# A gated decode kernel: the product with w1 takes the weights as the moving operand, and gelu works on rows

## The chip, the cores and the metric

The kernel runs on one core of one Trainium2 chip. The metric is the device time of one execution, in microseconds (us). Before the change it was 1337.64 us, the median of 3 runs (1337.64 to 1337.76).

## The reference

Two branches read the same two tokens and are mixed by a gate. Branch A is attention over a cache of 16384 positions and 32 heads. Branch B is a small mixer and an MLP.

```python
B, S, D = 2, 1, 1024            # one position per sequence
x = A_x
g = sigmoid((x * gate_w).sum(-1, keepdims=True))
# A: q = x @ wq; softmax(q K^T / sqrt(128)) V; @ wo      K and V: 268 MB each
# B:
h  = gelu(layernorm(x) @ w1)                  # w1: 1024 x 1024
g0..g3 = the four column blocks of h, each shifted by 1, -1, 2, -2 positions
hs = concatenate([g0, g1, g2, g3]) @ w2       # w2: 1024 x 1024
x1 = x + hs
b  = x1 + gelu(layernorm(x1) @ w3) @ w4
out = g * a + (1 - g) * b
```

With S = 1 every shift moves the only position out of the sequence, so all four blocks are zero, hs is zero, and h does not reach the output. The kernel computes h all the same, and then uses a zeroed tile in its place.

## The kernel before

Everything is streamed through one ring of three buffers of 64 KB per partition: the K and V tiles of the 32 attention steps, and between them the weights. One queue carries all of these loads. A load is issued when a ring buffer becomes free.

```python
NBIG = 3
big = ctx.enter_context(tc.tile_pool(name="big", bufs=NBIG))
# ... (cut)
def issue_ready():
    while xfers:
        ring, freed_by, load = xfers[0]
        used = ring_used[ring]
        if len(used) >= ring_size[ring] and used[-ring_size[ring]] not in done:
            return
        load()                       # nc.sync.dma_start(...), always the same queue
        used.append(freed_by)
        xfers.pop(0)
```

The work on one K tile begins with 16 transposes on VectorE (DVE), each followed by four matmuls on TensorE (PE).

```python
def qk_stage(i):
    # ... (cut)
    for m in range(NM):                                   # NM = 16
        T = t_tile([P, 2, CJ, 32], FP32)
        nc.vector.transpose(out=..., in_=Kw[:, m * CW : (m + 1) * CW]...)   # L325
        for v in range(4):
            nc.tensor.matmul(S[:], lhsT=z[...], rhs=Tb[:, v // 2, :, v % 2], ...)   # L333
```

The stage that the change touches runs once, after the fifth of the 32 attention steps. It takes w1 and w2 out of one ring buffer. The reader of the profile meets it as L513 (both products), L532 (the copy of h), L491 to L504 (gelu) and L442 (the residual's matmuls, which end the stage).

```python
def linear(key, actT):                       # weights stationary, two columns moving
    w = wt.pop(key)
    R, C = w.shape[1], w.shape[2] // P       # 8 and 8
    ps = misc_psum([P, C, B])
    for c in range(C):
        for r in range(R):
            nc.tensor.matmul(ps[:, c, :], lhsT=w[:, r, :]...[:, :, c], rhs=actT[:, r, :],
                             start=(r == 0), stop=(r == R - 1))
    return ps

def st_mix():
    layernorm(xT[:], xn1T[:])
    h1 = const.tile([P, KC, B], FP32, name="h1")
    nc.vector.tensor_copy(out=h1[:], in_=linear("w1", xn1T)[:])
    gelu(h1[:], hT[:], KC)                   # hT has no reader
    nc.vector.memset(shT[:], 0.0)
    # ... (cut: raises an error if more than one position)
    nc.vector.tensor_tensor(out=x1[:], in0=xT[:], in1=linear("w2", shT)[:], op=ALU.add)
    layernorm(x1[:], xn2T[:])                # rstd by a pow on GpSimd (POOL)
    start_out(x1[:])
```

Of the kernel before, what the change touches and what calls it, by code (L numbers as in the profile page):

```python
# [10 lines left out]
FP32 = mybir.dt.float32  # L11
BF16 = mybir.dt.bfloat16
ACTF = mybir.ActivationFunctionType
ALU = mybir.AluOpType
# [9 lines left out]
def kernel(  # L24
# [15 lines left out]
    nc = tc.nc  # L40
    P = nc.NUM_PARTITIONS
    B, Sq, D = A_x.shape
# [9 lines left out]
    KC = D // P  # L52
    FC = F // P
# [8 lines left out]
    const = ctx.enter_context(tc.tile_pool(name="const", bufs=1))  # L62
# [8 lines left out]
    def misc_psum(shape, dtype=FP32):  # L71
        return mps.tile(shape, dtype, tag="misc", name="misc")
# [4 lines left out]
    def t_tile(shape, dtype, name="T"):  # L77
        return tpool.tile(shape, dtype, tag="T", name=name)
# [6 lines left out]
    wt = {}  # L85
# [53 lines left out]
    def load_first():  # L139
# [12 lines left out]
        out=perm[:].rearrange("k (h a) -> k h a", a=4),  # L152
        in_=ident_f[:].rearrange("k (a h) -> k h a", a=4),
# [26 lines left out]
    for g in range(1, 4):  # L180
        nc.vector.tensor_tensor(
            out=osel_f, in0=osel_f, in1=ident_f[:, 40 * g : 40 * g + 8], op=ALU.add
# [9 lines left out]
        out=pick[:], in_=ident_f[:].rearrange("p (g w) -> p g w", w=32)[:, :, 0:B]  # L192
# [28 lines left out]
    omg_bc = const.tile([P, B], FP32)  # L221
# [21 lines left out]
    def group(g):  # L243
        return slice(32 * g, 32 * g + B)

    def zero_rows(ps, g, width):
        nc.tensor.matmul(
            ps[32 * g : 32 * g + 32, :],
            lhsT=perm[:, 0:32],
            rhs=zero[:].to_broadcast([P, width]),  # L250
            start=True,
            stop=False,
            skip_group_check=True,
        )
# [180 lines left out]
    def start_out(x1):  # L435
        for g in range(NQ):
            zero_rows(out_acc, g, QW)
        res = const.tile([P, KC, B], FP32, name="cen")
        nc.vector.tensor_tensor(out=res[:], in0=x1, in1=over_r(omg_bc[:]), op=ALU.mult)
        for c in range(KC):  # L440
            for g in range(NQ):
                nc.tensor.matmul(  # L442
                    out_acc[group(g), c:QW:KC],
                    lhsT=res[:, c, :],
                    rhs=ident_f[:, 32 * g : 32 * g + 32],
                    start=False,
                    stop=False,
                    skip_group_check=True,
                )
# [16 lines left out]
    def layernorm(src, dst):  # L466
        part = stat.tile([P, B], FP32, name="part")
        nc.vector.reduce_sum(out=part[:], in_=src.rearrange("p r b -> p b r"), axis=AX.X)
        mean = stat.tile([P, B], FP32, name="mean")
        nc.vector.tensor_scalar(  # L470
            out=mean[:], in0=total(part[:])[:], scalar1=1.0 / D, scalar2=None, op0=ALU.mult
        )
        cen = const.tile([P, KC, B], FP32, name="cen")
        nc.vector.tensor_tensor(out=cen[:], in0=src, in1=over_r(mean[:]), op=ALU.subtract)
        sq = const.tile([P, KC, B], FP32, name="cen_sq")
        nc.vector.tensor_tensor(out=sq[:], in0=cen[:], in1=cen[:], op=ALU.mult)
        part2 = stat.tile([P, B], FP32, name="part")
        nc.vector.reduce_sum(out=part2[:], in_=sq[:].rearrange("p r b -> p b r"), axis=AX.X)
        ve = stat.tile([P, B], FP32, name="mean")
        nc.vector.tensor_scalar(  # L480
            out=ve[:], in0=total(part2[:])[:], scalar1=1.0 / D, scalar2=LN_EPS, op0=ALU.mult, op1=ALU.add
        )
        rstd = stat.tile([P, B], FP32, name="rstd")
        nc.gpsimd.tensor_tensor(
            out=rstd[:], in0=ve[:], in1=neg_half[:].to_broadcast([P, B]), op=ALU.pow
        )
        nc.vector.tensor_tensor(out=dst, in0=cen[:], in1=over_r(rstd[:]), op=ALU.mult)

    def gelu(pre_f32, dst_bf, C, weight=None):
        sq = t_tile([P, C, B], FP32, "gelu")  # L490
        nc.vector.tensor_tensor(out=sq[:], in0=pre_f32, in1=pre_f32, op=ALU.mult)  # L491
        nc.vector.tensor_scalar(
            out=sq[:], in0=sq[:], scalar1=GELU_C1, scalar2=1.0, op0=ALU.mult, op1=ALU.add
        )
        nc.vector.tensor_tensor(out=sq[:], in0=sq[:], in1=pre_f32, op=ALU.mult)
        nc.scalar.activation(out=sq[:], in_=sq[:], func=ACTF.Tanh, scale=GELU_C0)
        nc.vector.tensor_scalar(
            out=sq[:], in0=sq[:], scalar1=1.0, scalar2=0.5, op0=ALU.add, op1=ALU.mult
        )
        if weight is not None:  # L500
            nc.vector.tensor_tensor(
                out=sq[:], in0=sq[:], in1=weight.unsqueeze(1).to_broadcast([P, C, B]), op=ALU.mult
            )
        nc.vector.tensor_tensor(out=dst_bf, in0=sq[:], in1=pre_f32, op=ALU.mult)  # L504

    def linear(key, actT):

        w = wt.pop(key)
        R, C = w.shape[1], w.shape[2] // P
# [3 lines that stand above are left out]
                nc.tensor.matmul(  # L513
                    ps[:, c, :],
                    lhsT=w[:, r, :].rearrange("k (p c) -> k p c", c=C)[:, :, c],
                    rhs=actT[:, r, :],
                    start=(r == 0),
                    stop=(r == R - 1),
                )
        return ps  # L520

    xn1T = const.tile([P, KC, B], BF16)
    hT = const.tile([P, KC, B], BF16)
    shT = const.tile([P, KC, B], BF16)
    x1 = const.tile([P, KC, B], FP32)
    xn2T = const.tile([P, KC, B], BF16)
    h2T = const.tile([P, FC, B], BF16)

    def st_mix():
        layernorm(xT[:], xn1T[:])  # L530
        h1 = const.tile([P, KC, B], FP32, name="h1")
        nc.vector.tensor_copy(out=h1[:], in_=linear("w1", xn1T)[:])  # L532
        gelu(h1[:], hT[:], KC)
        nc.vector.memset(shT[:], 0.0)
        for s in range(Sq):
            for blk, shift in enumerate((1, -1, 2, -2)):
                if 0 <= s - shift < Sq:
                    raise NotImplementedError("one position only")
        nc.vector.tensor_tensor(out=x1[:], in0=xT[:], in1=linear("w2", shT)[:], op=ALU.add)
        layernorm(x1[:], xn2T[:])  # L540
        start_out(x1[:])

    def st_up():
        h2 = t_tile([P, FC, B], FP32, "h2")
        nc.vector.tensor_copy(out=h2[:], in_=linear("w3", xn2T)[:])
        gelu(h2[:], h2T[:], FC, omg_bc[:])

    def st_down():
        w4 = wt.pop("w4")
# [4 lines left out]

    extra = {
        NT // 8: (lambda: load_rows(["w1", "w2"], [B_w1, B_w2]), st_mix),
        NT // 4: (lambda: load_rows(["w3"], [B_w3]), st_up),
    }
    xfers = [("big", "q", load_first)]
# [43 lines left out]
    for b, queue in enumerate((nc.sync, nc.scalar)):  # L603
        queue.dma_start(
            out=out[b].rearrange("s (g n) -> (s g) n", g=NQ), in_=rows[b : 96 + b + 1 : 32, :]
# [31 lines left out]
```

## Time and profile before

| | before |
|---|---|
| time | 1337.64 us |
| bytes read from HBM | 572.5 MB, 429 GB/s over the span |
| busy: PE, DVE | 60%, 57% |
| first product (64 pairs of weight load and matmul) | 3.96 us |
| gelu operation on DVE | 0.17 us each |
| DVE idle between this stage and the next K tile | 5.3 us |

These lines are from the page of before: the span, the busy time of each engine, the DMA row (busy tenths in 40 slices of the span), and the total read.

```profile
span 1335.9 us, 11948 instructions
...
PE 795.9 (60%) x5000; PEld 355.3 (27%) x5063; DVE 757.1 (57%) x998; ACT 26.8 (2%) x68; POOL 12.9 (1%) x40
...
DMA  9999999999999999999999999999999999999997
...
HBM read 572.53 MB, written 0.00 MB: 429 GB/s over the span
```

The DMA row is the one to read first. It stands at 90% or more in all slices but the last, while no engine is busy for much more than half of the span.

Next, the timeline of before around the stage. The columns are start, duration, engine, line, operation, output<-inputs, shape and count, and in brackets the idle time of the engine before it and what ended it. SPq is the queue on which loads are issued.

```profile
243.01 0.33 SPq L107 DMA_DIRECT2D Vn<-in_A_v_cache_dram  x1
...
249.16 3.96 PE L513 MATMUL misc<-xn1T,wt 128*128 128x2 bf16 x64 [1.24 <-DVE xn1T L487]
...
252.98 3.98 PE L513 MATMUL misc<-shT,wt 128*128 128x2 bf16 x64
253.15 0.17 DVE L532 COPY h<-misc 128x16 f32<-128x16 f32 x1 [3.91 <-PE misc L513]
...
256.99 0.33 SPq L96 DMA_DIRECT2D Kn<-in_A_k_cache_dram  x1
...
259.76 0.69 POOL L484 TENSOR_TENSOR rstd<-mean,neg_half 128x2 f32<-128x2 f32 x1 [10.86 <-DVE mean L480]
...
260.93 1.03 PE L442 MATMUL out_acc<-ident_f,cen 128*2 128x32 f32 x64 [1.02 <-DVE cen L439]
266.16 2.37 DVE L325 STREAM_TRANSPOSE T<-Kn 128x1024 f32<-128x1024 f32 x2 [5.29 <-DMA Kn<-in_A_k_cache_dram]
```

PE does the two products one after the other, then DVE adds the residual and normalises, and the residual's matmuls end at 261.96 (260.93 plus 1.03). Then DVE stands idle for 5.29 us until a K tile lands at 266.16. Also note the two loads of 8.4 MB: V was issued at 243.01 and K, into the buffer that w1 and w2 leave, at 256.99.

Last, the chain of waits of before in the same stretch (start, duration, what):

```profile
249.16 7.81 PE misc L513 x128
...
256.99 48.90 DMA Kn<-in_A_k_cache_dram
...
305.92 1.25 DVE T L325
```

The chain puts 7.81 us of these very matmuls before a load of 48.90 us. But 8.4 MB take 19.2 us at 436 GB/s, a rate that many of the 40 slices of this page show.

### The profile page before, as it was taken

How to read it: one execution, taken by the hardware profiler on the slowest of the kernel's cores; microseconds unless marked ns; L12 is line 12 of the kernel's file. 1: busy time of each engine (PE TensorE's matmuls, PEld its weight loads, DVE VectorE, ACT ScalarE, POOL GpSimd, SP SyncE). 2: the span in 40 equal slices, each digit the busy share in tenths (PEclk: the TensorE clock that was granted, in tenths of full speed). 3: DMA queues.
4: the chain of work that ended last, by engine and by line, in shares of the span. 5: the costliest groups of instructions: out<-in, count | busy, mean ns of one | idle time of the engine just before them, and what ended most of it. 6: DMA issues, size and time to landing (the moment at which the load reports that its data are there). Idle time of an engine off the chain costs nothing.

```text
span 1335.9 us, 11948 instructions
## 1 busy us (share of the span) xinstructions
PE 795.9 (60%) x5000; PEld 355.3 (27%) x5063; DVE 757.1 (57%) x998; ACT 26.8 (2%) x68; POOL 12.9 (1%) x40
## 2 busy tenths in 40 slices
PE   2576655676656665555666555566655556665564
PEld 0223222432225222222222222232222222222232
DVE  1677665366652665555666555566655556665540
ACT  0000000000000000000000000000000000000000
POOL 0000000000000000000000000000000000000000
PEclk9788777688776877778887777888777788877775
DMA  9999999999999999999999999999999999999997
GB/s 409 436 438 434 421 438 428 437 438 432 428 435 435 439 424 434 430 436 438 438 427 432 430 432 438 436 432 432 432 436 438 427 430 432 438 436 438 424 423 302
DMA packets 12726, 573.31 MB, mean 429 GB/s; under 512 B 1784, under 2 KB 1792, under 8 KB 2560
## 3 DMA queue, kind: packets, MB, share of 16 engines
q1 hardware_dynamic: 12664, 572.54, 99.2%
q8 instruction: 40, 0.66, 0.2%
q14 instruction: 14, 0.11, 0.0%
q10 hardware_dynamic: 8, 0.00, 0.0%
HBM read 572.53 MB, written 0.00 MB: 429 GB/s over the span
## 4 chain that ended last, share of the span: by engine, by line
PE 26%; DVE 25%; DMA 23%; another core or an unknown queue 12%; issue 11%; ACT 1%; SPq 0%; ACTq 0%; POOL 0%
DVE T L325 19%; PE S L333 15%; DMA Kn<-in_A_k_cache_dram 13%; PE O L377 7%; DMA wt<-in_B_w_dram 4%; DMA Vn<-in_A_v_cache_dram 3%; DMA wo<-in_A_wo_dram 3%; PE misc L212 2%; DVE Os L392 2%; PE misc L513 2%; ACT Pr L361 1%; DVE PT L365 1%; DVE mx L354 1%; PE misc L400 1%
## 5 line engine op out<-in xcount | busy, mean ns | idle before, releaser
L333 PE MATMUL S<-T,z 128*128 128x512 bf16 x1985 | 582.1, 421 | 334.3 <-DVE T L325 312.2
L325 DVE STREAM_TRANSPOSE T<-Kn 128x1024 f32<-128x1024 f32 x512 | 612.5, 1230 | 261.2 <-DMA Kn<-in_A_k_cache_dram 209.6
L333 PEld LDWEIGHTS <-z 128*128 128x128 bf16 x2048 | 210.8, 104 | 692.3 <-issue 529.8
L377 PE MATMUL O<-Vn,PT 128*32 128x512 bf16 x2048 | 121.4, 390 | 3.1 <-DMA Vn<-in_A_v_cache_dram 3.1
L377 PEld LDWEIGHTS <-PT 128*32 128x32 bf16 x2048 | 74.2, 141 | 49.2 <-issue 20.3
L388 DVE TENSOR_SCALAR Os<-O,xmask 128x128 f32<-128x128 f32 x32 | 11.2, 350 | 101.2 <-PE O L377 101.2
L212 PE MATMUL misc<-rs,ones_f 128*128 128x2 f32 x64 | 17.9, 349 | 79.1 <-DVE rs L408 79.1
L361 ACT ACTIVATE Pr<-S,nb 128x512 bf16<-128x512 f32 x32 | 22.0, 687 | 1203.4 <-DVE nb L356 1165.8
L344 DVE TENSOR_REDUCE m<-S 128x1 f32<-128x512 f32 x32 | 22.1, 692 | 36.9 <-PE S L333 36.9
L400 PE MATMUL misc<-asel,Os 128*128 128x2 f32 x64 | 12.4, 264 | 51.0 <-DVE Os L392 51.0
L365 DVE STREAM_TRANSPOSE PT<-Pr 128x512 bf16<-128x512 bf16 x32 | 22.7, 711 | 28.7 <-ACT Pr L361 28.7
L212 PEld LDWEIGHTS misc<-rs,ones_f 128*128 128x128 f32 x64 | 16.1, 312 | 84.0 <-issue 81.2
L392 DVE SCALAR_TENSOR_TENSOR Os<-O,xmask,Os 128x128 f32<-128x128 f32 x96 | 33.7, 351 | 3.4
L400 PEld LDWEIGHTS misc<-asel,Os 128*128 128x128 f32 x64 | 9.7, 191 | 65.2 <-DVE Os L392 60.9
L212 PE MATMUL misc<-mdiag,ones_f 128*128 128x128 f32 x64 | 15.5, 325 | 17.1 <-DVE mdiag L347 17.1
L354 DVE TENSOR_REDUCE mx<-misc 64x1 f32<-64x64 f32 x64 | 14.2, 222 | 19.1 <-PE misc L212 18.6
L513 PEld LDWEIGHTS <-wt 128*128 128x128 bf16 x352 | 22.3, 172 | 9.7 <-DMA wt<-in_B_w_dram 8.4
L301 POOL TENSOR_TENSOR z<-qsel,own 128x32 bf16<-128x32 bf16 x32 | 10.8, 338 | 1207.3 <-PE S L333 1177.4
L513 PE MATMUL misc<-xn2T,wt 128*128 128x2 bf16 x224 | 14.4, 202 | 8.2 <-DMA wt<-in_B_w_dram 8.2
L412 DVE RECIPROCAL rinv<-misc 128x2 f32<-128x2 f32 x32 | 5.5, 170 | 22.6 <-PE misc L212 22.6
L269 PE MATMUL misc<-wt,xT 128*2 128x512 bf16 x64 | 5.8, 540 | 19.7 <-DVE xT L257 19.7
L602 DVE CAST rows<-out_acc 128x256 bf16<-128x256 f32 x1 | 0.4, 423 | 29.6 <-PE out_acc L426 29.6
(82 smaller groups left out, 104.6 us busy)
## 6 DMA issues: line engine op xcount, KB each, us to landing
Vn<-in_A_v_cache_dram SPq DMA_DIRECT2D x2, 4096.0 KB, 47.1
wt<-in_B_w_dram SPq DMA_DIRECT2D x1, 7168.0 KB
w<-in_B_w_dram SPq DMA_DIRECT2D x4, 1792.0 KB, 31.4
wo<-in_A_wo_dram SPq DMA_DIRECT2D x6, 1024.0 KB, 33.2
wt<-in_B_w_dram SPq DMA_DIRECT2D x2, 2048.0 KB, 37.3
wo<-in_A_wo_dram SPq DMA_DIRECT2D x2, 512.0 KB, 18.7
wo<-in_A_wo_dram SPq DMA_DIRECT2D x4, 256.0 KB, 12.7
Kn<-in_A_k_cache_dram SPq DMA_DIRECT2D x32, 52.3
```

Of the source, the lines that this page charges most:

```text
L212: nc.tensor.matmul(ps[:], lhsT=ones_f[:], rhs=src, start=True, stop=True)
L325: nc.vector.transpose(out=T[:].rearrange("p w j s -> p j w s"), in_=Kw[:, m * CW : (m + 1) * CW].rearrange("p (j w e) -> p j w e", w=2, e=32),
L333: nc.tensor.matmul(S[:], lhsT=z[:, v, NM - 1 - m : NM - 1 - m + P], rhs=Tb[:, v // 2, :, v % 2], start=(m == 0 and v == 0), stop=(m == NM ...
L344: nc.vector.reduce_max(out=m[:], in_=S[:], axis=AX.X)
L354: nc.vector.reduce_max(out=mx[pa, :], in_=mall[pa, pa], axis=AX.X)
L361: nc.scalar.activation(out=Pr[:], in_=S[:], func=ACTF.Exp, bias=nb[:], scale=scale, accum_out=rs[:])
L365: nc.vector.transpose(out=PT[:], in_=Pr[:])
L377: nc.tensor.matmul(O[32 * g : 32 * g + 32, :], lhsT=PT[:, m : CJ * 32 : 16], rhs=V[:, j0 : j0 + 4, :], start=(m == 0), stop=(m == NM - 1),)
L388: nc.vector.tensor_scalar(out=Os[:], in0=Ox, scalar1=xmask[:, 0:1], scalar2=None, op0=ALU.mult)
L392: nc.vector.scalar_tensor_tensor(out=Os[:], in0=Ox, scalar=xmask[:, x : x + 1], in1=Os[:], op0=ALU.mult, op1=ALU.add,)
L400: nc.tensor.matmul(oc[:], lhsT=Os[:], rhs=asel[:], start=True, stop=True)
L513: nc.tensor.matmul(ps[:, c, :], lhsT=w[:, r, :].rearrange("k (p c) -> k p c", c=C)[:, :, c], rhs=actT[:, r, :], start=(r == 0), stop=(r == ...
```

## The change

The intent is to swap the roles of the operands in the product with w1: the two columns of activations are loaded as weights, and w1 streams past as the moving operand, 512 columns at a time, in two column groups of the array (32 columns each, as `group(g)` in the kernel places them). So 64 loads of full 128x128 weights become 16 loads of two columns. The result, in PSUM (the memory that matmuls write to), then lies on rows (two partitions of each group, 512 columns), and gelu works on that shape.

```diff
-    def gelu(pre_f32, dst_bf, C, weight=None):
-        sq = t_tile([P, C, B], FP32, "gelu")
+    def gelu(pre_f32, dst_bf, weight=None):
+        shape = list(pre_f32.shape)
+        sq = t_tile(shape, FP32, "gelu")
 ... (the weight is broadcast to this shape; the second call of gelu only drops its third argument)
-    hT = const.tile([P, KC, B], BF16)
+    h_rows = const.tile([P, D // 2], BF16)
 ...
     def st_mix():
         layernorm(xT[:], xn1T[:])
-        h1 = const.tile([P, KC, B], FP32, name="h1")
-        nc.vector.tensor_copy(out=h1[:], in_=linear("w1", xn1T)[:])
-        gelu(h1[:], hT[:], KC)
+        w1 = wt.pop("w1")
+        HW = D // 2
+        ps = misc_psum([P, HW])
+        for g in range(2):
+            zero_rows(ps, g, HW)
+        for r in range(KC):
+            for g in range(2):
+                nc.tensor.matmul(
+                    ps[group(g), :],
+                    lhsT=xn1T[:, r, :],
+                    rhs=w1[:, r, g * HW : (g + 1) * HW],
+                    start=False,
+                    stop=(r == KC - 1),
+                    skip_group_check=True,
+                )
+        h1 = t_tile([P, HW], FP32, "h1")
+        nc.vector.tensor_copy(out=h1[0:64, :], in_=ps[0:64, :])
+        gelu(h1[0:64, :], h_rows[0:64, :])
         nc.vector.memset(shT[:], 0.0)
```

More of the change, by code (lines that the diff above doesn't have):

```diff
@@ L501, in gelu @@
             nc.vector.tensor_tensor(
-                out=sq[:], in0=sq[:], in1=weight.unsqueeze(1).to_broadcast([P, C, B]), op=ALU.mult
+                out=sq[:], in0=sq[:], in1=weight.unsqueeze(1).to_broadcast(shape), op=ALU.mult
             )
@@ L545, in st_up @@
         nc.vector.tensor_copy(out=h2[:], in_=linear("w3", xn2T)[:])
-        gelu(h2[:], h2T[:], FC, omg_bc[:])
+        gelu(h2[:], h2T[:], omg_bc[:])
     def st_down():
```

## The prediction

> **What bounds the kernel now.** One DMA queue that is never empty. The page shows 572.5 MB read in 1335.9 us, 429 GB/s, with the DMA row at 9 tenths in 39 of 40 slices, while PE is busy 60% and DVE 57%. The DMA issues listed in order show one K and one V load of 8.4 MB about every 39 us; at the usual 436 GB/s the pair takes 38.5 us, so the period is the transfer time.
>
> **What the change touches.** One stage, run once, at 244 to 262 us (timeline). Its result h is never read: with one position all shifted blocks are zero, and the second product uses the zeroed shT. Only order on PE and DVE, and the moment the w1/w2 buffer is free, can carry an effect.
>
> **PE.** Removed: 64 weight loads of 128 columns with 64 two-column matmuls, 3.96 us (249.16 to 253.1, 62 ns a pair). Added: 16 matmuls of 512 columns with two-column weights, in two column groups, and 2 zeroing matmuls. The q projection at the start does the same with four groups: the timeline shows one round of four every 0.43 us until the clock rises. Groups run side by side, so I expect 8 rounds x 0.43 = 3.4 us at the granted clock of 0.50 that this stage has (table of windows). The zeroing matmuls fit into the 1.2 us in which PE waits for xn1T. PE gains about 0.3 to 0.5 us; the second product then ends near 256.6 instead of 257.0.
>
> **DVE and ACT.** Seven operations of 16 columns, 0.17 to 0.22 us each, become 512 columns on 64 partitions. The copy out of PSUM: 0.69 us, as the 128x512 cast does in the q projection. For fp32 tensor_tensor the Trainium skill, "VectorE: DVE Perf Modes", section "The TRN2 errata", gives (N+151)/0.96 ns. It agrees with this trace (56 columns: 216 by the formula, 198 to 216 measured), so three of them at 512 columns are an estimated 0.69 us each; two tensor_scalars about 0.43; tanh about 0.69, as the exp of 512 columns. DVE work rises from 1.2 to about 3.6 us. About 1.4 us of it (copy, square) falls into the 2.4 us in which DVE waits for the second product; the rest now sits between the steps of the second layernorm. This chain, ending with the residual's matmuls at 262.0, should end between 261.8 and 263.5.
>
> **How much is critical.** None. The next K tile lands at 266.16, where DVE had idled 5.3 us: 3 to 4 us of slack remain. The chain of waits does put 7.8 us of these matmuls before a 48.9 us K load, which looks critical. It isn't: at its issue at 257.0, the K load of 238.3 and the V load of 243.0 were still in flight, so it queued about 29 us (48.9 less 19.5 of its own transfer). Issuing it a little earlier or later moves nothing.
>
> **Prediction.** 1337.6 us, range 1335.6 to 1339.6. Faster by over 2%: 0.01; within 2%: 0.98; slower by over 2%: 0.01.
>
> **What would show it.** Right: the first DVE transposes after the stage begin near 266 again, after 3 to 5 us idle that a K load ends; GB/s and DMA rows unchanged; w1 matmuls 3.2 to 3.8 us; gelu operations 0.4 to 0.7 us. Wrong: those transposes start after the K tile has landed, held by PE or DVE; or the column groups run one after the other (7 us).
>
> **What would make it wrong.** The DMA rate depending on how many loads are queued; or the groups serialising AND the layernorm delayed over 4 us; even then under 5 us, 0.4%.

## The result, and the profile after

The changed kernel takes 1337.45 us (median of 6 runs, 1337.38 to 1337.61), and before took 1337.59 us in the runs that go with it. The ratio is 0.9999, with a 95% interval from 0.9986 to 1.0012: no change. A ratio here is the mean time of one kernel's fast runs over that of the other's fast runs of the same rounds, so it is not quite the ratio of the medians that are quoted.

The same lines from the page of after:

```profile
span 1335.6 us, 11856 instructions
...
PE 796.7 (60%) x4954; PEld 353.6 (26%) x5017; DVE 759.0 (57%) x998; ACT 27.2 (2%) x68; POOL 13.3 (1%) x40
...
DMA  9999999999999999999999999999999999999997
...
HBM read 572.53 MB, written 0.00 MB: 429 GB/s over the span
```

Rate, DMA row and bytes are as before. The timeline of after around the stage:

```profile
242.83 0.33 SPq L107 DMA_DIRECT2D Vn<-in_A_v_cache_dram  x1
...
247.66 0.61 PE L247 MATMUL misc<-zero,perm 128*32 128x512 bf16 x2
...
248.97 3.58 PE L539 MATMUL misc<-wt,xn1T 128*2 128x512 bf16 x16 [0.70 <-DVE xn1T L487]
...
252.48 4.01 PE L514 MATMUL misc<-shT,wt 128*128 128x2 bf16 x64
252.59 0.68 DVE L548 COPY h<-misc 64x512 f32<-64x512 f32 x1 [3.53 <-PE misc L539]
253.31 0.68 DVE L492 TENSOR_TENSOR gelu<-h 64x512 f32<-64x512 f32 x1
256.52 0.33 SPq L96 DMA_DIRECT2D Kn<-in_A_k_cache_dram  x1
...
259.33 0.68 DVE L505 TENSOR_TENSOR h_rows<-gelu,h 64x512 bf16<-64x512 f32 x1
259.49 1.07 POOL L484 TENSOR_TENSOR rstd<-mean,neg_half 128x2 f32<-128x2 f32 x1 [10.78 <-DVE mean L480]
...
261.04 1.03 PE L442 MATMUL out_acc<-ident_f,cen 128*2 128x32 f32 x64 [1.39 <-DVE cen L439]
265.90 2.37 DVE L325 STREAM_TRANSPOSE T<-Kn 128x1024 f32<-128x1024 f32 x2 [4.92 <-DMA Kn<-in_A_k_cache_dram]
```

The stage itself did change. The zeroing matmuls ran in the gap before xn1T was ready. The first product took 3.58 us in place of 3.96. The copy and the first gelu operation took 0.68 us each in place of 0.17, inside the wait for the second product. The residual's matmuls end at 262.07, against 261.96 before, and after 4.92 us of idle DVE the K tile lands at 265.90. One record is longer that was not expected to be: the pow on POOL took 1.07 us in place of 0.69.

The chain of waits of after:

```profile
248.97 3.58 PE misc L539 x16
252.55 3.96 PE misc L514 x64
...
256.52 49.26 DMA Kn<-in_A_k_cache_dram
...
305.80 1.26 DVE T L325
```

The K load was issued 0.47 us earlier than before, and its wait in the chain grew by 0.36 us (48.90 to 49.26). The tile landed at 305.80, and at 305.92 before, as good as the same moment. What PE gave, the queue took.

### The profile page after: what moved, and what is told of

The parts are those of the page before. It is cut to its first block, busy times and chain, and to the rows that moved or that the text cites. A ratio compares the mean times of both kernels' runs of the same rounds, so it can differ in the third digit from the quotient of the medians.

```text
span 1335.6 us, 11856 instructions
## 1 busy us (share of the span) xinstructions
PE 796.7 (60%) x4954; PEld 353.6 (26%) x5017; DVE 759.0 (57%) x998; ACT 27.2 (2%) x68; POOL 13.3 (1%) x40
## 4 chain that ended last, share of the span: by engine, by line
DVE 25%; PE 25%; DMA 23%; issue 13%; another core or an unknown queue 12%; ACT 1%; SPq 0%; ACTq 0%; POOL 0%
DVE T L325 19%; PE S L333 14%; DMA Kn<-in_A_k_cache_dram 13%; PE O L377 7%; DMA wt<-in_B_w_dram 4%; DMA Vn<-in_A_v_cache_dram 3%; DMA wo<-in_A_wo_dram 3%; PE misc L212 2%; DVE Os L392 2%; PE misc L514 1%; ACT Pr L361 1%; DVE PT L365 1%; DVE mx L354 1%; PE misc L400 1%
## 5 line engine op out<-in xcount | busy, mean ns | idle before, releaser
L365 DVE STREAM_TRANSPOSE PT<-Pr 128x512 bf16<-128x512 bf16 x32 | 22.8, 711 | 28.7 <-ACT Pr L361 28.7
L514 PEld LDWEIGHTS <-wt 128*128 128x128 bf16 x288 | 18.2, 171 | 9.2 <-DMA wt<-in_B_w_dram 8.3
L269 PE MATMUL misc<-wt,xT 128*2 128x512 bf16 x64 | 5.8, 541 | 19.5 <-DVE xT L257 19.5
```

The lines of the kernel that those rows point to most:

```text
L365: nc.vector.transpose(out=PT[:], in_=Pr[:])
L514: nc.tensor.matmul(ps[:, c, :], lhsT=w[:, r, :].rearrange("k (p c) -> k p c", c=C)[:, :, c], rhs=actT[:, r, :], start=(r == 0), stop=(r == ...
```

## The experiments

Theory A: the queue of loads sets the time; it is never empty, and this stage lies in slack, on the engines (about 5 us) and in the queue (over 20 us). Rival B: the stage is on the chain of waits, as the chain seems to say, and the gain of the product was given back by the longer DVE operations. A second, smaller question is why the pow on POOL grew. All edits below are to the changed kernel. All ten runs gave the reference's outputs.

### Without the product and its gelu, w1 still loaded

```diff
-        w1 = wt.pop("w1")
-        ... (product, copy and gelu)
+        wt.pop("w1")
```

> The kernel after without its first product and its gelu (both dead work); w1 is still loaded. Theory A (the queue of loads sets the time, this stage lies in slack): the second product ends some 3.5 us earlier, the chain of the second layernorm ends near 257.5 instead of 262.1, the next K load is issued near 253 instead of 256.5, and yet the first K transposes still begin at 265.9 (within 0.4) and the time stays within 0.4 us of before. Rival B (the stage is on the chain, and a gain on PE of 0.5 us was given back on DVE): the time falls by 3.5 us (the product alone) or more, to 1334 or below.

Measured: 1337.54 us against 1337.50 for before in the same rounds, ratio 0.9999 (0.9983 to 1.0016). The timeline of this run:

```profile
248.13 3.97 PE L514 MATMUL misc<-shT,wt 128*128 128x2 bf16 x64
...
252.14 0.33 SPq L96 DMA_DIRECT2D Kn<-in_A_k_cache_dram  x1
...
256.13 1.03 PE L442 MATMUL out_acc<-ident_f,cen 128*2 128x32 f32 x64 [1.01 <-DVE cen L439]
266.24 2.37 DVE L325 STREAM_TRANSPOSE T<-Kn 128x1024 f32<-128x1024 f32 x2 [10.16 <-DMA Kn<-in_A_k_cache_dram]
```

The second product starts at 248.13 and the stage ends at 257.16, some 5 us earlier than in after. The K load was issued at 252.14. DVE then idles 10.16 us, and the transposes begin at 266.24, when the K tile lands, as always. The second product ended 4.4 us earlier than in after and not 3.5 as expected, since it no longer waits for the first layernorm. A stage that is 5 us shorter gained nothing. Rival B is out, and so is any idea that gain and loss cancelled: there was no gain to cancel.

### w1 not loaded either; then neither w1 nor w2

```diff
-  NT // 8: (lambda: load_rows(["w1", "w2"], [B_w1, B_w2]), st_mix),
+  NT // 8: (lambda: load_rows(["w2"], [B_w2]), st_mix),       # first run, product and gelu left out
```
```diff
+  NT // 8: (None, st_mix),                                    # second run, no load for this stage
     def st_mix():
-        ... (first layernorm, product, gelu, second product)
-        nc.vector.tensor_tensor(out=x1[:], in0=xT[:], in1=linear("w2", shT)[:], op=ALU.add)
+        nc.vector.tensor_copy(out=x1[:], in_=xT[:])
```

> As the run without the product, and w1 is not loaded either: 2.10 MB less of 572.5. Theory A: the time falls by what these bytes cost at 429 to 438 GB/s, 4.8 to 4.9 us, to 1332.7 (1332.2 to 1333.2). Rival B: the load is hidden, and the time is that of the run without the product but with the load.

> Both dead products go, and neither w1 nor w2 is loaded: 4.19 MB less. x1 is a copy of x, which is what adding a product with zeros gives. Theory A: 9.6 to 9.8 us less than before, near 1327.9 (1327.2 to 1328.6), with the same rate of 429 GB/s over the span and the right result; DVE and PE busy time hardly change. Rival B: the time falls by the 8 us of the two products at most, and not in step with the bytes.

Measured: 1332.71 us without w1 (ratio 0.9965, 0.9950 to 0.9980) and 1327.89 us without both (ratio 0.9928, 0.9913 to 0.9943), against 1337.50 for before. These are 4.79 us and 9.61 us less. Dividing the bytes left out by them gives 2.10 MB / 4.79 us = 438 GB/s and 4.19 MB / 9.61 us = 436 GB/s, which is the rate of the queue. (These are medians; the slowest and fastest of the runs allow 416 to 448 GB/s for the second.) The page of the run without both:

```profile
span 1326.0 us, 11728 instructions
...
PE 798.2 (60%) x4931; PEld 346.8 (26%) x4931; DVE 754.2 (57%) x984; ACT 26.6 (2%) x67; POOL 12.2 (1%) x39
...
HBM read 568.33 MB, written 0.00 MB: 429 GB/s over the span
```

PE and DVE are as busy as before, the rate is the same 429 GB/s, and the span is shorter by the time of the bytes. This is also the version that beats both kernels, by 0.7%. It is exact for one position only, which the kernel requires anyway, and it assumes finite weights. Leaving out the work on w1 without its bytes gave nothing; leaving out the bytes gave all. (The second product was left out only together with the bytes of w2.)

### The product done 5, 13, 17 and 25 times

To measure the slack, the stage was made longer on purpose. The repeats add into the same PSUM tile, so h is wrong; nothing reads it.

```diff
+        for rep in range(5):                # 13, 17, 25
             for r in range(KC):
                 for g in range(2):
                     nc.tensor.matmul(ps[group(g), :], ...,
-                        stop=(r == KC - 1),
+                        stop=(rep == 4 and r == KC - 1),
```

> The first product is done 5 times into the same PSUM tile (h is wrong on purpose; nothing reads it), which holds PE, then DVE, and the buffer of w1 and w2, longer: 4 more times, each 1.8 us at full clock to 3.5 us at half, so 7 to 10 us more. Theory A: the 4.9 us of idle DVE before the next K tile are used up and the transposes begin 2 to 5 us late, at 268 to 271, but the queue of loads never runs empty: the time stays within 0.5 us of before. Rival B (the stage is on the chain): 7 to 10 us longer.

> 13 products: 12 more, about 22 us longer in this stage. Theory A: the transposes begin about 17 us late, near 283; the K load is issued near 278, before the V load ahead of it has landed (about 285.4), and the next V load near 304, before that K load lands (305.8): the queue just never runs empty, and the time rises by 0 to 3 us. Rival B: 22 us longer.

> 25 products: 24 more, about 43 us longer. Theory A: now the K load is issued near 300, some 14 us after the V load ahead of it has landed, so the queue runs empty, and again for 4 us before the next V load[...]: the time rises by 16 to 24 us, about half of the delay put in, and the transfers show a gap between about 286 and 301. Rival B: 43 us longer. If a stage of this kind costs nothing even here, theory A is wrong too.

> 17 products: 16 more, 6.9 us longer than the run with 13, by the 1.73 us that the runs with 13 and 25 show for one. The run with 25 showed the queue empty from 283.2 us on, so the true slack of the K load is 283.2 less 256.5, 26.7 us, and not the 29 us of the prediction. Theory A with that figure: the K load is issued near 284.2, a little too late; with about 1 us between issue and first bytes the queue stands empty for 1 to 3 us, and again for 1 to 4 us before the next V load, issued near 309. The time rises by 2 to 7 us over before, to 1339.5 to 1344.5: between the 0.5 us of 13 products and the 16.5 us of 25. If the time rises in proportion to the delay beyond 13, without the knee, it is 1343 (16.0 us x 4/12 = 5.3 us more), which this run cannot tell from it; the gap in the transfers can: none if the queue is not what counts.

Measured, with the issue times and first transposes read from the timelines:

| products | K load issued | first transposes | next V load issued | queue empty (table of windows) | time less before |
|---|---|---|---|---|---|
| 1 (after) | 256.5 | 265.9 | 287.1 | never | -0.1 |
| 5 | 265.3 | 269.6 | 290.6 | never | 0.0 |
| 13 | 277.2 | 281.6 | 302.3 | never, but 393 GB/s in 302 to 307 (after: 419) | +0.5 |
| 17 | 285.8 | 290.2 | 311.5 | 284 to 286 and 307 to 312 | +8.1 |
| 25 | 298.0 | 302.4 | 319.2 | 283 to 298 and 318 to 320 | +16.5 |

The ratios to before are 1.0000 (0.9985 to 1.0015), 1.0003 (0.9988 to 1.0018), 1.0057 (1.0041 to 1.0074) and 1.0129 (1.0112 to 1.0146).

With 5 products the idle time of DVE is already used up. This line is the first transpose after the stage in that run; it has no bracket, so DVE went straight from the stage to it, 3.7 us after the K tile would have been taken in after:

```profile
269.61 2.36 DVE L325 STREAM_TRANSPOSE T<-Kn 128x1024 f32<-128x1024 f32 x2
```

It cost nothing. The lost time is made up behind a queue that still has loads in it. With 13 products the transposes begin 15.7 us late, and the time is 0.5 us longer, less than the spread of that run (1337.43 to 1338.47). With 25 products the queue at last runs empty. This is the table of windows of that run: length, busy time of each engine (and instructions), PE's clock, share of the DMA engines, GB/s.

```profile
core 0: us, PE busy (x) PEld busy (x) DVE busy (x) ACT busy (x) POOL busy (x), PEclk, DMA share, GB/s
278.00:283.00 5.00, 5.00 (x50) 1.93 (x46) 0.00 (x0) 0.00 (x0) 0.00 (x0) 1.00 0.96 410
283.00:298.00 15.00, 14.96 (x166) 8.05 (x162) 1.37 (x3) 0.00 (x0) 0.00 (x0) 0.95 0.01 5
298.00:318.00 20.00, 19.38 (x169) 7.75 (x170) 16.17 (x25) 0.63 (x1) 1.07 (x1) 0.78 1.01 421
318.00:320.00 2.00, 2.00 (x11) 0.67 (x10) 1.86 (x2) 0.00 (x0) 0.00 (x0) 1.00 0.04 8
320.00:330.00 10.00, 6.27 (x25) 2.43 (x23) 7.75 (x15) 0.58 (x1) 0.33 (x1) 1.00 1.04 419
```

For 15 us almost nothing is moved (5 GB/s), and for 2 us more (8 GB/s) before the next V load. The two gaps make 17 us; the time rose by 16.5. The run with 17 products has two gaps as well:

```profile
284.00:286.00 2.00, 1.79 (x30) 1.71 (x29) 0.17 (x2) 0.00 (x0) 0.00 (x0) 1.00 0.00 0
...
307.00:312.00 5.00, 4.93 (x27) 1.61 (x27) 4.17 (x4) 0.00 (x0) 0.00 (x0) 1.00 0.00 0
```

Counted whole, they make 7 us, and with the parts of the neighbouring slices (66 GB/s from 283 to 284 and from 305 to 307) the rise of 8.1 us fits. It was expected to be 2 to 7 us, so this forecast missed by 1.1 us: the K load was issued at 285.8 and not near 284.2, and the next V load at 311.5 and not near 309. In the builds with 17 and 25 products the scheduler also put part of the matmuls with V among those with K, which shifts when each buffer comes free; so these two are not exactly the same program with a longer wait. Rival B had 43 us more at 25 products, where the K load was issued 41.5 us later; 16.5 us were measured. The delay counts only from where the queue is empty.

The run with 25 products also corrects a number. The queue ran dry shortly after 283 (single slices of 1 us show the last bytes between 283 and 284), not near 286, as the prediction's 29 us of waiting would have it. The records come in bursts (in full flow a slice of 1 us shows anything from 0 to 1049 GB/s), so this edge is good to 1 or 2 us only. The step that was too large is "48.9 less 19.5 of its own transfer". A load's own time is longer than the moving of its bytes: the DMA view gives 22.8 us from issue to landing for the K load that the run with 25 products issued into the empty queue, and 23.1 us for the one with 17. So the wait in the queue was 48.9 less 22.8, some 26 us, which fits the edge: 283.2 less the issue in after, 256.5, is 26.7 us, and the first bytes came almost 1 us after an issue. The 29 us are the time until the V load ahead has landed: in the run with 25 products it landed 43.0 us after its issue at 243.43, at 286.4, some 3 us after the last bytes that the slices show.

### Both halves in one column group

```diff
-        ps = misc_psum([P, HW])
-        for g in range(2): zero_rows(ps, g, HW)
+        ps2 = [misc_psum([P, HW]) for _ in range(2)]
+        for g in range(2): zero_rows(ps2[g], 0, HW)
 ...
-                    ps[group(g), :],
+                    ps2[g][group(0), :],
 ...
-        nc.vector.tensor_copy(out=h1[0:64, :], in_=ps[0:64, :])
+        for g in range(2):
+            nc.vector.tensor_copy(out=h1[32 * g : 32 * g + 32, :], in_=ps2[g][0:32, :])
```

> The kernel after with both halves of the first product in the same column group (two PSUM tiles, partitions 0 and 1 of each), so that no two matmuls can run side by side. The prediction holds if the 16 matmuls now take 5 to 7 us (0.43 us each at half clock, 0.22 once the clock rises) in place of 3.58, so the second product ends 1.5 to 3.5 us later; DVE then also has two copies of 512 columns. If the column groups bring nothing, it stays at 3.6 us. The first K transposes still begin within 0.5 us of 266 and the time stays within 0.5 us of before.

Measured in one look: 1337.48 us, before 1337.50. The timeline:

```profile
249.19 5.88 PE L539 MATMUL misc<-wt,xn1T 128*2 128x512 bf16 x16 [0.28 <-DVE xn1T L487]
...
262.64 0.41 DVE L498 TENSOR_SCALAR gelu<-gelu 64x512 f32<-64x512 f32 x1
262.80 0.80 POOL L484 TENSOR_TENSOR rstd<-mean,neg_half 128x2 f32<-128x2 f32 x1 [13.87 <-DVE mean L480]
...
265.99 2.37 DVE L325 STREAM_TRANSPOSE T<-Kn 128x1024 f32<-128x1024 f32 x2 [1.43 <-DMA Kn<-in_A_k_cache_dram]
```

The 16 matmuls took 5.88 us in place of 3.58, with the same shapes and count. The timelines show how: in after, weights are loaded for two matmuls every 0.43 us, here for one. (This run also writes two PSUM tiles and not one; that alone was not tried.) So the two column groups do run side by side, which is what makes the changed product a little shorter than the old one; in one group it would be longer (5.88 against 3.96). The transposes still begin at 265.99, after 1.43 us of idle time.

### The pow on POOL: the last multiply left out, or read from PSUM

```diff
-        gelu(h1[0:64, :], h_rows[0:64, :])
+        gelu(h1[0:64, :], None)                               # first run: no last multiply
+        gelu(h1[0:64, :], h_rows[0:64, :], last=ps[0:64, :])  # second run: its second operand from PSUM
```

> The kernel after without the last multiply of the first gelu (675 ns on DVE, its result is dead). Theory P (the second pow of rstd on GpSimd took 1.07 us and not 0.69 because this multiply, with two operands in SBUF, was running): pow back to 0.69 to 0.71 us, xn2T some 0.35 us earlier, the residual's matmuls end near 261.7. Rival Q (the pow is late for another reason, such as the load or its own variation): it still takes about 1.07 us. Either way the time stays within 0.5 us of before.

> The kernel after with the last multiply of the first gelu reading h from its PSUM tile and not from the SBUF copy: the same operation, of about the same length (0.65 to 0.75 us), at about the same moment, but with one operand in SBUF. Theory P (two SBUF operands on DVE held up the pow on GpSimd): pow back to 0.69 to 0.71 us even while the multiply runs. Rival Q1 (any DVE operation of this length there delays it): still 1.0 to 1.1 us. The time stays within 0.5 us of before.

Measured in one look each: 1337.42 and 1337.53 us. Without the multiply:

```profile
259.60 0.69 POOL L484 TENSOR_TENSOR rstd<-mean,neg_half 128x2 f32<-128x2 f32 x1 [10.39 <-DVE mean L480]
```

With the multiply, its second operand in PSUM (misc in place of h):

```profile
259.72 0.67 DVE L505 TENSOR_TENSOR h_rows<-gelu,misc 64x512 bf16<-64x512 f32 x1
259.88 0.69 POOL L484 TENSOR_TENSOR rstd<-mean,neg_half 128x2 f32<-128x2 f32 x1 [10.78 <-DVE mean L480]
```

The pow is back to 0.69 us in both. In the second, a multiply of the same length runs at the same moment, starting 0.16 us before the pow as in after, and does not hold it up; only the place of one operand differs. This is what the Trainium skill states in "SBUF — State Buffer", section "Who interferes with whom": a DVE instruction with two SBUF inputs contends with a GpSimd instruction that reads SBUF, since its second input comes through a shared interface. (SBUF is the on-chip memory that the engines read and write.) These runs agree: 1.07 us with two SBUF inputs, 0.69 with one. The others support them: with 5, 13, 17 and 25 products this pow begins beside the same multiply and takes 1.07 us each time, and the first pow of after, beside a transpose on DVE with one SBUF input, takes 0.70. The same section lists tensor_scalar among the operations that can take the shared pair. In the run with one column group the pow began during such an operation, and it took 0.80 us; that this operation was the cause was not tried.

## Why the prediction was right

- "One DMA queue that is never empty": shown. The time follows the bytes (the time saved is that of the bytes left out at 436 to 438 GB/s), not the work, and rises only where the windows show an empty queue.
- "How much is critical. None": shown by the run without the product, in which the stage was 5 us shorter, and by 5 and 13 products, in which it was 9 to 21 us longer, all at 1337.4 to 1337.9 us.
- The product: 3.4 us for the rounds was predicted, 3.2 to 3.8 us given for its record, and 3.58 measured. The second product was to end near 256.6 and ended at 256.49. That the groups run side by side was shown by the run with one group.
- DVE: 0.69 us each was estimated for the copy and the multiplies, and 0.68 measured; 0.43 for the tensor_scalars, and 0.41 measured. The Trainium skill's formula, (N+151)/0.96 ns from "VectorE: DVE Perf Modes", section "The TRN2 errata", gives 691 ns for 512 columns, where the trace of after has 675 to 683. The chain was to end between 261.8 and 263.5, and ended at 262.07.
- Too large: 29 us of queueing, where some 26 us were found. The transfer of 19.5 us was taken off the 48.9, and not the 22.8 us that a load takes by itself from issue to landing. The conclusion did not hang on it.
- Missed: the prediction looked at DVE for the cost in the second layernorm and overlooked POOL. The multiply made the pow 0.38 us longer. From the end of the second product to the end of the stage the chain grew from 5.00 to 5.58 us, so most of the growth was not DVE's own. That the end still lay in the range is in part luck: without the pow's delay it would have come near 261.7, a little before the range (the run without the multiply ended its stage at 261.80).
- Also too strict: it named transposes that start after the K tile has landed as a sign of being wrong. With 5 products they did so, at no cost, because the queue has slack of its own behind the idle time of DVE. For the same reason the worst case that it named, up to 5 us, was no threat: with 13 products the transposes began 15.7 us late, at a cost of 0.5 us.

## What to carry to other kernels

Where one queue of loads is always full, as here, an engine's work counts only once it makes the queue run dry. Before believing a chain of waits that ends in a long load, take from that wait what a load of the size needs by itself from issue to landing (22.8 us here): what is left is slack. In such a kernel time is bought with bytes: ask first which bytes the output does not need, and only then how the arithmetic is laid out. Swapping the operands of this thin product cost PE nothing because the column groups were used (3.58 us for 3.96), but it made the elementwise operations after it several times longer (0.68 us for 0.17), so check what runs beside them, on POOL too.

## What the Trainium skill lacked or had wrong

- "Perfetto Trace Analysis", sections "Identifying Dependency Chains" and "What "DMA-bound" means", do not say that a wait for a load can be mostly time in the queue, nor how to measure the slack (the page says elsewhere only that a DMA that looks fast may still be waiting). Here a load of 8.4 MB showed as 48.9 to 49.3 us in the chain, where one issued into an empty queue took 22.8 to 23.1; delaying its issue by 8.7 and 20.7 us cost 0.0 and 0.5 us.
- "DMA: Bandwidth & Descriptors", section "Where 436 GB/s comes from", says that for HBM to SBUF the HBM side, about 358 GB/s, binds, and leaves out there the condition that other passages of the skill state, two cores of a pair streaming at once. This kernel on one core did not show that limit: 429 GB/s over the span, and 436 to 438 GB/s by the bytes left out, close to the page's fabric figure of 435.
- "SBUF — State Buffer", section "Who interferes with whom", has the contention, says that the second one blocks until the first is done and names two ratios (6.8 and 1.5 times slower), but not what this adds to an operation that starts when part of the first is left. Two cases here: 0.52 us of the multiply were left when the pow started, and it took 0.38 us longer; 0.25 us of the tensor_scalar were left, and it took 0.11 us longer. Both are 0.14 us less than what was left. Spans on POOL are rough, and two cases make no rule.
- "VectorE: DVE Perf Modes" calls (N+151)/0.96 ns exact at N = 512, for additions; the multiplies of after, on 64 partitions, came out 1 to 2% shorter, 675 to 683 ns against 691.
